# Turning y by transposes and taking two steps' router logits from four column groups

## The chip, the cores and the metric

The kernel runs on one core of a Trainium2 chip. The metric is the device time of one launch in microseconds (us); lower is better. The engines named below are PE (TensorE matmul; PEld is its weight load), DVE (VectorE), ACT (ScalarE), POOL (GpSimd) and SP (SyncE, which issues most DMAs here). Each engine works through its own queue strictly in the order in which the program was traced.

## The reference

An outer-product recurrence (the attention half) feeds a router with two experts of eight per token (the mixture half). All data are float32.

```python
# attention: B, H, S, D = 4, 8, 768, 48
f = 1 / (1 + exp(-f_logit))
for t in range(S):
    state = f[:, :, t, :, None] * state + einsum('bhd,bhe->bhde', k[:, :, t], v[:, :, t])
    y[:, :, t] = einsum('bhd,bhde->bhe', q[:, :, t], state)
x = y.transpose(0, 2, 1, 3).reshape(B * S, H * D)          # 3072 tokens x 384
# router: E = 8
noisy = x @ w_gate + log1p(exp(x @ w_noise)) * noise        # both weights 384 x 8
top2, weights = two largest of noisy, softmax over the two
# experts, hidden 1024
out[t] = sum over the two experts e of weight * (relu(x[t] @ w1[e]) @ w2[e])
```

## The kernel before, in words

**Attention.** The sequence is cut into 6 chunks of 128 tokens (`NCH`, `C`); with 4 batches this gives 24 steps, numbered n = 0 to 23. A step holds all 8 heads as 4 pairs (`HP`); a head has 48 features, padded to 64 (`DP`), so that a pair fills 128 partitions. A step's work is split into stages: `forget` (transpose f on PE, exp and log on ACT), `summed` (a running sum on DVE, tile `L`), `decays` (two exponentials on ACT), `scaled` (transpose q and k on PE, multiply on DVE), `scores` (transpose k back, score products on PE, mask on DVE, tile `A`), `output` (products `y`, new state) and `features`. The main loop runs the stages of different steps in turn, software-pipelined: iteration i does, in this order, `forget(i+3)`, `scaled(i+1)`, `scores(i)`, `summed(i+2)`, `output(i-1)`, `decays(i+2)`, `features(i-2)`. `in_order` pins each engine's queue to this order of tracing.

**Features before the change** (line 627 on). `output` leaves y with features on the partitions and tokens along the free side; ACT copies it out of the accumulation banks to `yT` (line 607). `features` multiplies each pair's 128 x 128 block of `yT` by `w_rt`, a 128 x 112 matrix for each pair: 96 columns of an identity (they turn y to token order) and 16 columns of router weights. One bank `xp` thus holds the turned x and four partial logits. DVE adds the four partial logits into `lg` (line 630), ACT copies the 384 columns of x to `xs` (line 632), and SP writes `xs` to `x_rows` in DRAM (line 633), from which tokens are later gathered by expert. The write is put into SP's queue in the `output` stage of the next iteration, behind the loads of f, q, k and v that the earlier stages of that iteration issue. `xs` has three buffers.

**Loads.** f, q, k and v go to rings of slots in SBUF (5, 4, 4 and 6 slots), several steps ahead: `scaled(n)` issues q and k of step n+3, `scores(n)` issues v of step n+3, `forget(n)` issues f of step n+4. From step 9 to 16 each iteration also issues a part of the first experts' weights.

**Router.** After the fourth step of a chunk c, `route(c)` is started: a chain of small operations on ACT and DVE, some of them between two of the loop's stages (`next(router)`), which finds the two best experts and each token's place in its expert's list (`sloti`, line 707). A small product on PE, `rk` (lines 697, 698), counts tokens ahead. Then POOL writes the list entries into DRAM, 8 indirect DMAs for each chunk (line 711).

**Hand-over.** In program order on POOL, the 8 list writes of the fourth chunk (c = 3, steps 12 to 15) are followed by the first gather of tokens (line 885), whose rows PE turns (`xgp`, line 922) before the first expert's products (line 977) can begin. The rest of the kernel is the experts' work: 8 experts in 24 groups of 256 tokens and five small blocks, with the first and second layers by fast matrix-product schemes.

**Banks.** Six accumulation banks go round among all uses of `one_bank`; a new use waits until the use six before it has been read.

Of the kernel before, what the change touches and what calls it, by code (L numbers as in the profile page):

```python
# [10 lines left out]
F32 = mybir.dt.float32  # L11
# [5 lines left out]
AX = mybir.AxisListType  # L17
ALU = mybir.AluOpType
# [314 lines left out]
def kernel(  # L333
# [38 lines left out]
    nc = tc.nc  # L372
    B, H, S, D = q.shape
    N, DM = out.shape
    E = moe_w_gate.shape[1]
    FF = moe_w1.shape[2]
    C = 128
    NCH = S // C
    HP = H // 2
    DP = 64  # L380
    KO = DM // 128
    FO = FF // 128
# [26 lines left out]
    const = ctx.enter_context(tc.tile_pool(name="const", bufs=1))  # L409
# [5 lines left out]
    wk = attention.enter_context(tc.tile_pool(name="wk", bufs=2))  # L415
# [3 lines left out]
    def one_bank(name):  # L419
        turns.append(turns.pop(0))  # L420
        return turns[-1].tile([128, 512], F32, tag="one", name=name)
# [5 lines left out]
    ident = const.tile([128, 128], F32, tag="ident", name="ident")  # L427
# [56 lines left out]


    XW = 2 * D
    w_rt = const.tile([128, HP, XW + 2 * E], F32, tag="w_rt", name="w_rt")
    noise = const.tile([128, NCH, B, E], F32, tag="noise", name="noise")

    def load_router(part):  # L490

        if part < 2:
            for i, w in ((part, (moe_w_gate, moe_w_noise)[part]),):
                for odd in range(2):
                    for par in range(2):
                        nc.gpsimd.dma_start(out=w_rt[par * DP:par * DP + D, odd::2, XW + i * E:XW + (i + 1) * E],
                                          in_=w.rearrange("(a o r d) e -> o r d a e", o=2, r=2, d=D)[odd, par ^ odd])
        else:
            c = part - 2
            nc.sync.dma_start(out=noise[:, c], in_=moe_noise.rearrange("(b s) e -> s b e", b=B)[c * C:(c + 1) * C])  # L500
# [15 lines left out]
    def cols(hp):  # L516
        return slice(hp * C, (hp + 1) * C)
# [62 lines left out]
    def output(n):  # L580
        c, b = n // B, n % B
# [18 lines left out]
        if c:  # L600
            for hp in range(HP):
                for par in range(2):
                    nc.tensor.matmul(at(hp, par), lhsT=state[b][rows(par), hp, :],  # L603
                                     rhs=qP[n][rows(par), cols(hp)], start=False, stop=(hp >= HP - 2))
        yT[n] = wk.tile([128, 2, HP // 2 * C], F32, tag="yT", name=f"yT_{n}")
        for odd in range(2):
            nc.scalar.copy(yT[n][:, odd, :], y[odd][:, 0:HP // 2 * C])  # L607
        if c == NCH - 1:
            return

# [4 lines left out]
        if c == 0:  # L615
            nc.gpsimd.tensor_tensor(new, dsv, end, ALU.mult)
        else:
            mid = wk.tile([128, HP, DP], F32, tag="mid", name=f"mid_{n}")
            nc.gpsimd.tensor_tensor(mid, dsv, state[b], ALU.add)
            nc.gpsimd.tensor_tensor(new, mid, end, ALU.mult)  # L620
        state[b] = new

    def features(n):
        c, b = n // B, n % B
        xp = one_bank(f"xp_{n}")[:, 0:HP * (XW + 2 * E)].rearrange("t (a w) -> t a w", a=HP)
        for hp in range(HP):
            nc.tensor.matmul(xp[:, hp, :], lhsT=yT[n][:, hp % 2, cols(hp // 2)], rhs=w_rt[:, hp, :], start=True, stop=True)  # L627
        if b == 0:
            lg[c] = rt.tile([128, B, 2 * E], F32, tag="lg", name=f"lg_{c}", bufs=NCH)
        nc.vector.tensor_reduce(lg[c][:, b, :], xp[:, :, XW:].rearrange("t a e -> t e a"), axis=AX.X, op=ALU.add)  # L630
        xs = wk.tile([128, HP, XW], F32, tag="xs", name=f"xs_{n}", bufs=3)
        nc.scalar.copy(xs, xp[:, :, 0:XW])
        xw.append(lambda: nc.sync.dma_start(out=x_rows[n * C:(n + 1) * C, :], in_=xs.rearrange("t a w -> t (a w)")))


    def route(c):
        def t(shape, tag, dtype=F32):
# [129 lines left out]
    def nearly_enough():  # L767
        total = one_bank("total_c")[:, 0:E]
        nc.tensor.matmul(total, lhsT=ones, rhs=upto[NCH - 2][:, :, B], start=True, stop=True)
        yield  # L770
        nc.vector.scalar_tensor_tensor(short, in0=total[0:1, 0:1], scalar=511.5, in1=short, op0=ALU.is_lt, op1=ALU.max)
        yield
# [646 lines left out]
    clamp(1, nc.vector)  # L1419
    pad("v")  # L1420
    nc.gpsimd.memset(w_rt, 0.0)
    for odd in range(2):
        for r in range(2):
            nc.gpsimd.tensor_copy(w_rt[:, odd::2, r * D:(r + 1) * D],
                                  ident[:, (r ^ odd) * DP:(r ^ odd) * DP + D].unsqueeze(1).broadcast_to((128, HP // 2, D)))
    for part in range(2):
        load_router(part)
    clamp(3)
# [67 lines left out]
    for i in range(-3, NS + 2):  # L1496
# [5 lines left out]
        for stage, lag in order:  # L1502
            n = i - lag
            if not 0 <= n < NS:
                continue
            stage(n)
            if stage is forget:
                for m in () if n < 2 else (n + 3,) if n < 5 else (n + 3, n + 4) if n == 5 else (n + 4,):
                    load("f", m)
# [48 lines left out]
        if n >= 0 and n % B == B - 1:  # L1558
            c = n // B
            router = chain(router, route(c))  # L1560
            n_routed = c + 1
            if c == HALF - 1:
                router = chain(router, enough())
                first_pairs = first_loads()
            if c == NCH - 1:
                router = chain(router, nearly_enough(), plan(), beyond())
    while NCH - 1 not in begun:
        next(router)
    for _ in first_pairs:
# [96 lines left out]
```

## Time and profile before

| | |
|---|---|
| median of three runs | 619.19 us (618.45 to 619.34) |
| profiled execution, its own time | 617.76 us |
| its span from first to last instruction | 615.7 us |
| PE busy | 602.0 us, 98% |
| DVE, ACT, POOL busy | 451.9, 377.8, 290.9 us (73, 61, 47%) |
| granted TensorE clock, mean | 0.996 |

The profile is one execution. Its own time lies 2.1 us above its span (launch and end around it), and 1.4 us below the median of the timed runs. Attention takes about the first 158 us. "Busy" counts instructions in flight; idle time of an engine is put down to the event that ended it, which is inferred.

### The profile page before, as it was taken

The numbers are of one execution on the slowest core, as the hardware profiler recorded it, in microseconds if no ns is written. First come the engines' busy times: TensorE is split into PE (matmuls) and PEld (weight loads), VectorE is DVE, ScalarE is ACT, GpSimd is POOL, SyncE is SP. The second block draws the span as 40 slices with busy tenths as digits, with TensorE's granted clock in tenths as the row PEclk, the third lists the DMA queues.
The fourth block names the chain that finished last, engine by engine and source line by source line (L and its number), as shares of the span: only waits on it lengthen the run. The fifth ranks groups of instructions, "written<-read, shape, count | busy, mean of one in ns | idle before, by whom it ended". The sixth has DMA issues, their size and how long they took to land.

```text
span 615.7 us, 13343 instructions
## 1 busy us (share of the span) xinstructions
PE 602.0 (98%) x4830; PEld 553.0 (90%) x4830; DVE 451.9 (73%) x1056; ACT 377.8 (61%) x920; POOL 290.9 (47%) x316
## 2 busy tenths in 40 slices
PE   8999999999999999999999999999999999999995
PEld 7999998887999988998898899889988998998994
DVE  7777878778665488878777778787777777877840
ACT  6877676754222587667666755775577567647611
POOL 7724688878887550451062335414540624242032
PEclk9999999999999999999999999999999999999998
DMA  9999887996973874686489279839874893361024
GB/s 185 187 200 213 174 173 158 206 190 162 327 193 87 142 195 138 142 165 212 138 196 263 65 197 170 259 136 185 159 215 128 199 250 84 82 136 20 2 27 56
DMA packets 186219, 98.79 MB, mean 160 GB/s; under 512 B 150736, under 2 KB 179408, under 8 KB 186144
## 3 DMA queue, kind: packets, MB, share of 16 engines
q1 hardware_dynamic: 173968, 78.59, 51.2%
q0 software_dynamic: 12176, 19.25, 17.2%
q8 instruction: 40, 0.66, 0.4%
q14 instruction: 35, 0.29, 0.2%
HBM read 69.68 MB, written 19.62 MB: 145 GB/s over the span
## 4 chain that ended last, share of the span: by engine, by line
PE 82%; DMA 6%; issue 3%; POOL 3%; ACT 2%; DVE 2%; POOLq 0%; ACTq 0%
PE y L1218 27%; PE E L1052 8%; PE D L1052 8%; PE B L1052 6%; PE C L1052 6%; PE hp L977 5%; PE y L1162 3%; DMA x_rows<-xs 3%; PE sc L574 3%; PE y L592 3%; PE xp L627 2%; PE A L1052 2%; DMA xg<-hs_b 2%; PE fp L534 1%; POOL lists L711 1%
## 5 line engine op out<-in xcount | busy, mean ns | idle before, releaser
L1099 POOL DMA_INDIRECT out_dram<-ys,slots x48 | 91.1, 1898 | 216.0 <-DVE ys L1224 167.6
L1218 PE MATMUL y<-qk_all,f_all 128*128 128x192 f32 x504 | 88.8, 326 | 0.0
L1218 PEld LDWEIGHTS y<-qk_all,f_all 128*128 128x128 f32 x504 | 83.1, 190 | 0.0
L885 POOL DMA_INDIRECT xg<-x_rows,slots x48 | 52.5, 1093 | 36.0 <-DMA slots<-lists 18.8
L1060 ACT ACTIVATE hs_b<-hs_b 128x256 f32<-128x256 f32 x140 | 58.5, 418 | 6.9 <-DVE hs_b L1064 5.2
L1224 DVE SCALAR_TENSOR_TENSOR ys<-y,slots,ys 128x192 f32<-128x192 f32 x63 | 26.1, 415 | 49.1 <-PE y L1218 16.4
L1218 PE MATMUL y<-w,hs_b 128*128 128x192 f32 x336 | 61.5, 326 | 0.0
L711 POOL DMA_INDIRECT lists<-entry,sloti x48 | 52.8, 1101 | 8.7 <-issue 7.4
L1218 PEld LDWEIGHTS y<-w,hs_b 128*128 128x128 f32 x336 | 56.0, 190 | 0.4
L1267 ACT ACTIVATE ys<-y,slots 128x192 f32<-128x192 f32 x21 | 8.9, 421 | 59.5 <-PE y L1218 55.7
L577 DVE TENSOR_TENSOR A<-sc,causal 128x1024 f32<-128x1024 f32 x24 | 29.3, 1221 | 9.0 <-PE sc L574 8.5
L607 ACT COPY yT<-y 128x256 f32<-128x256 f32 x48 | 15.7, 376 | 29.8 <-PE y L603 21.4
L1057 ACT COPY hs_a<-D 128x256 f32<-128x256 f32 x77 | 28.5, 371 | 8.4 <-PE D L1052 4.5
L1218 PE MATMUL y<-qk_all,hs_b 128*128 128x192 f32 x168 | 31.5, 331 | 0.3 <-ACT ys L1239 0.2
L936 ACT COPY planes<-xg 128x768 uint16<-128x768 uint16 x36 | 29.6, 825 | 3.4 <-DMA xg<-x_rows,slots 2.8
L1218 PE MATMUL y<-w,f_all 128*128 128x192 f32 x168 | 31.3, 329 | 0.0
L548 DVE TENSOR_TENSOR_SCAN L<-f,cap 128x512 f32<-128x512 f32 x24 | 29.3, 1221 | 1.4 <-ACT cap L543 1.4
L1057 ACT COPY hs_a<-E 128x256 f32<-128x256 f32 x63 | 23.5, 372 | 10.8 <-PE E L1052 9.5
L1218 PEld LDWEIGHTS y<-qk_all,hs_b 128*128 128x128 f32 x168 | 27.4, 190 | 3.0 <-issue 2.1
L528 POOL TENSOR_SCALAR f_all<-f_all 128x384 f32<-128x384 f32 x21 | 26.4, 1257 | 5.0 <-DMA f_all<-in_f_logit_dram 2.7
L1087 DVE TENSOR_TENSOR f_all<-hs_b 128x512 f32<-128x512 f32 x42 | 28.7, 682 | 0.0
L1218 PEld LDWEIGHTS y<-w,f_all 128*128 128x128 f32 x168 | 27.6, 190 | 0.7
(273 smaller groups left out, 1593.4 us busy)
## 6 DMA issues: line engine op xcount, KB each, us to landing
w<-in_moe_w_dram SPq DMA_DIRECT2D x12, 1536.0 KB
w_q<-in_moe_w_dram SPq DMA_DIRECT2D x10, 1536.0 KB
w<-in_moe_w_dram SPq DMA_DIRECT2D x16, 384.0 KB
f_all<-in_f_logit_dram SPq DMA_DIRECT2D x24, 192.0 KB
qk_all<-in_q_dram SPq DMA_DIRECT2D x24, 192.0 KB
qk_all<-in_k_dram SPq DMA_DIRECT2D x24, 192.0 KB
v_all<-in_v_dram SPq DMA_DIRECT2D x24, 192.0 KB
x_rows<-xs SPq DMA_DIRECT2D x24, 192.0 KB
```

The source lines that it names most:

```text
L548: nc.vector.tensor_tensor_scan(L[n], data0=logf[n], data1=cap[n % 2].rearrange("d a t -> d (a t)"), initial=0.0, op0=ALU.add, op1=ALU.min)
L577: nc.vector.tensor_tensor(A[n].rearrange("j r (a i) -> j (r a) i", i=C), sc.rearrange("j r (a i) -> j (r a) i", i=C), causal.unsqueeze(1). ...
L711: into = nc.gpsimd.indirect_dma_start(out=lists, out_offset=bass.IndirectOffsetOnAxis(ap=sloti[:, r, b:b + 1], axis=0), in_=entry[:, c, b, ...
L885: nc.gpsimd.indirect_dma_start(out=xg[p][:, s, :], out_offset=None, in_=x_rows[0:(known(p) + (p == 1 and s)) * B * C], in_offset=bass.Indi ...
L936: nc.scalar.copy(planes[p][:, s], by_halves(p)[:, s * 2 * DM:(s + 1) * 2 * DM].rearrange("t (d h) -> t h d", h=2))
L977: nc.tensor.matmul(hp[:, o, :], lhsT=w1[home(k)][:, i, (fo + o) * 128:(fo + o + 1) * 128], rhs=rows_of(k)[:, i, :], start=(i == 0), stop=( ...
L1052: nc.tensor.matmul(banks[name, j], lhsT=half_of(x, k)[:, j * 128:(j + 1) * 128], rhs=half_of(y, k), start=first, stop=True, skip_group_che ...
L1057: nc.scalar.copy(at(to, j), banks[more[0], j])
L1060: nc.scalar.activation(at(to, j), at(y, j), AF.Relu, scale=-1.0 if more[0][0] == "-" else 1.0)
L1087: nc.vector.tensor_tensor(sm[which], x, y, op)
L1099: into = nc.gpsimd.indirect_dma_start(out=out, out_offset=bass.IndirectOffsetOnAxis(ap=slots[p][:, s, 2:3], axis=0), in_=ys[s], in_offset= ...
L1218: nc.tensor.matmul(to, lhsT=x[:, o, :], rhs=y[:, o, :], start=(start and o == 0), stop=(o == FH - 1), skip_group_check=not start)
```

## The change

The turning matrix leaves `w_rt`, which shrinks to 32 columns for each pair (16 of weights, 16 of zeros). y is turned by four PE transposes for each step. The logits of an odd step and the even one before it are computed together: four products, one for each pair, with `w_rt` as the stationary operand and 256 columns of `yT` as the moving one; the four go to four groups of 32 partitions of one bank, `both`. DVE copies these 128 x 256 partial logits to SBUF (`parts`, a slice of `hs_a` that attention does not use otherwise); PE turns them back with two transposes, in `logits()`, which the main loop calls after the next stage that it runs; DVE then adds the pairs. `yT` becomes one tile for two steps. ACT writes `xs` in two copies. The buffer `mid` goes from two to one.

```diff
-    w_rt = const.tile([128, HP, XW + 2 * E], F32, tag="w_rt", name="w_rt")
+    EP = 32
+    w_rt = const.tile([128, HP, EP], F32, tag="w_rt", name="w_rt")
...
-        yT[n] = wk.tile([128, 2, HP // 2 * C], F32, tag="yT", name=f"yT_{n}")
+        if n % 2 == 0:
+            yT[n // 2] = wk.tile([128, HP, 2, C], F32, tag="yT", name=f"yT_{n}")
         for odd in range(2):
-            nc.scalar.copy(yT[n][:, odd, :], y[odd][:, 0:HP // 2 * C])
+            nc.scalar.copy(yT[n // 2][:, odd::2, n % 2, :], y[odd][:, 0:HP // 2 * C].rearrange("d (m t) -> d m t", t=C))
...
-            mid = wk.tile([128, HP, DP], F32, tag="mid", name=f"mid_{n}")
+            mid = wk.tile([128, HP, DP], F32, tag="mid", name=f"mid_{n}", bufs=1)
...
     def features(n):
         c, b = n // B, n % B
-        xp = one_bank(f"xp_{n}")[:, 0:HP * (XW + 2 * E)].rearrange("t (a w) -> t a w", a=HP)
-        for hp in range(HP):
-            nc.tensor.matmul(xp[:, hp, :], lhsT=yT[n][:, hp % 2, cols(hp // 2)], rhs=w_rt[:, hp, :], start=True, stop=True)
         if b == 0:
             lg[c] = rt.tile([128, B, 2 * E], F32, tag="lg", name=f"lg_{c}", bufs=NCH)
-        nc.vector.tensor_reduce(lg[c][:, b, :], xp[:, :, XW:].rearrange("t a e -> t e a"), axis=AX.X, op=ALU.add)
+        if n % 2:
+            both = one_bank(f"lg_{n}")
+            for hp in range(HP):
+                nc.tensor.matmul(both[hp * EP:(hp + 1) * EP, 0:2 * C], lhsT=w_rt[:, hp, :],
+                                 rhs=yT[n // 2][:, hp].rearrange("d b t -> d (b t)"), start=True, stop=True)
+            parts = hs_a[:, FO - 1, :]
+            nc.vector.tensor_copy(parts, both[:, 0:2 * C])
+            back.append((n, both, parts))
+        xp = one_bank(f"xp_{n}")
+        for hp in range(HP):
+            nc.tensor.transpose(xp[:, cols(hp)], yT[n // 2][:, hp, n % 2, :], ident)
         xs = wk.tile([128, HP, XW], F32, tag="xs", name=f"xs_{n}", bufs=3)
-        nc.scalar.copy(xs, xp[:, :, 0:XW])
+        blocks = xp.rearrange("t (m x d) -> t m x d", x=4, d=DP)
+        for to in range(2):
+            nc.scalar.copy(xs.rearrange("t (m o) (r d) -> t m o r d", o=2, r=2)[:, :, :, to, :],
+                           blocks[:, :, 0:4:3, 0:D] if to == 0 else blocks[:, :, 1:3, 0:D])
...
+    def logits():
+        n, both, parts = back.pop(0)
+        for b in range(2):
+            nc.tensor.transpose(both[:, (2 + b) * C:(3 + b) * C], parts[:, b * C:(b + 1) * C], ident)
+        nc.vector.tensor_reduce(lg[n // B][:, n % B - 1:n % B + 1, :],
+                                both[:, 2 * C:].rearrange("t (b a w) -> t b w a", b=2, w=EP)[:, :, 0:2 * E], axis=AX.X, op=ALU.add)
...
-    for odd in range(2):
-        for r in range(2):
-            nc.gpsimd.tensor_copy(w_rt[:, odd::2, r * D:(r + 1) * D],
-                                  ident[:, (r ^ odd) * DP:(r ^ odd) * DP + D].unsqueeze(1).broadcast_to((128, HP // 2, D)))
...
+            waiting = bool(back)
             stage(n)
+            if waiting:
+                logits()
...
+    logits()
     while NCH - 1 not in begun:
```

## Rows read from the trace of the kernel before

**Rows 1.** The page: busy time of each engine, its share of the span, instructions.

```profile
PE 602.0 (98%) x4830; PEld 553.0 (90%) x4830; DVE 451.9 (73%) x1056; ACT 377.8 (61%) x920; POOL 290.9 (47%) x316
```

**Rows 2.** The chain of work, one whole step in the middle of attention: start, length, engine, tile, line.

```profile
48.58 1.09 PE sc L574 x16
...
51.16 0.60 PE y L603 x16
51.76 1.07 PE xp L627 x8
52.83 0.44 PE fp L534 x4
...
54.58 1.09 PE sc L574 x16
```

**Rows 3.** The chain of work later, among the experts: four column groups of 32, stationary 128 x 32, moving 128 x 256, 12 products as 24 instructions.

```profile
301.75 1.43 PE hp_q L1317 x24
```

**Rows 4.** The chain of work from 96 to 160 us, the pieces that lead to the hand-over.

```profile
119.58 5.39 DMA x_rows<-xs
...
125.05 0.48 ACT xs L632
125.53 0.12 ACT ex L667
...
131.45 0.31 DVE sloti L707
...
132.03 1.01 POOL lists L711
...
145.14 3.73 DMA xg<-x_rows,slots
...
149.01 0.52 PE xgp L922 x3
```

**Rows 5.** Timeline of ACT, the copies to `xs` of steps 12, 14 and 16: start, length, then in brackets the idle time before and what ended it.

```profile
98.78 0.50 ACT L632 COPY xs<-xp 128x384 f32<-128x384 f32 x1
...
111.48 0.48 ACT L632 COPY xs<-xp 128x384 f32<-128x384 f32 x1 [0.77 <-DMA x_rows<-xs]
...
125.05 0.48 ACT L632 COPY xs<-xp 128x384 f32<-128x384 f32 x1 [1.47 <-DMA x_rows<-xs]
```

**Rows 6.** The tile `xs`, its copies and its writes to DRAM, up to 114 us: durations in ns (least, median, most), first and last start in us.

```profile
L632 ACT COPY xs<-xp x15: 468/497/499, 25.8 to 111.5; 128x384 f32<-128x384 f32 x15
L633 SPq DMA_DIRECT2D x_rows<-xs x13: 343/869/2542, 31.7 to 113.3; - x13
```

**Rows 7.** Loads of q issued up to 114 us, and transposes of q (four for a step) up to then.

```profile
L522 SPq DMA_DIRECT2D qk_all<-in_q_dram x20: 526/720/1908, 1.9 to 107.1; - x20
L534 PE MATMUL qp<-ident,qk_all x76: 272/273/328, 8.0 to 110.5; 128*128 128x128 f32 x76
```

**Rows 8.** Timeline of SP's queue around the write of step 13 to `x_rows`.

```profile
118.79 0.70 SPq L522 DMA_DIRECT2D v_all<-in_v_dram  x1
119.58 0.66 SPq L633 DMA_DIRECT2D x_rows<-xs  x1
```

**Rows 9.** Waits of SP's queue from 0 to 165 us, the largest entry: total, times, longest.

```profile
SPq L522 <- PE y L603: 6.8, 5, 2.7
```

**Rows 10.** Two stretches: length, busy time (and count) of PE, PEld, DVE, ACT, POOL, then the granted clock, the DMA engines' busy share, GB/s.

```profile
25.00:98.00 73.00, 72.39 (x1039) 66.13 (x1037) 55.33 (x131) 53.38 (x144) 43.76 (x64) 1.00 0.89 186
118.00:131.00 13.00, 12.58 (x180) 11.12 (x181) 9.84 (x35) 8.67 (x24) 10.29 (x16) 1.00 1.02 224
```

**Rows 11.** Timeline of DVE from 129 us: the running sum, the logits of step 17, and the router's operation behind them.

```profile
129.29 1.21 DVE L548 TENSOR_TENSOR_SCAN L<-f,cap 128x512 f32<-128x512 f32 x1
130.42 0.20 DVE L630 TENSOR_REDUCE lg<-xp 128x16 f32<-128x64 f32 x1
130.53 0.18 DVE L701 TENSOR_TENSOR at<-rk,list_of 128x32 f32<-128x32 f32 x1
```

**Rows 12.** Single lines with their durations in ns: a copy out of a bank by DVE, 384 and a sum of 192 columns; a reduction over 128 columns; a copy out of a bank by ACT, 256 columns, and a scaled one of 192.

```profile
L923 DVE COPY xt_a<-xgp x2: 545/546/548, 150.3 to 152.6; 128x384 f32<-128x384 f32 x2
L1192 DVE TENSOR_TENSOR mid<-mid,y x3: 353/354/354, 174.6 to 216.4; 128x192 f32<-128x192 f32 x3
L794 DVE TENSOR_REDUCE ex_plan<-past_plan x1: 285/285/285, 175.1 to 175.1; 128x16 f32<-128x128 f32 x1
L607 ACT COPY yT<-y 128x256 f32<-128x256 f32 x48 | 15.7, 376 | 29.8 <-PE y L603 21.4 <-PE kp L534 3.4 <-PE qp L534 3.1
L1243 ACT ACTIVATE ys<-y,slots 128x192 f32<-128x192 f32 x21 | 8.8, 421 | 9.4 <-PE y L1218 9.3
```

**Rows 13.** Timeline of PE from 127 us (start, length in flight, line), and at the hand-over.

```profile
127.45 1.63 PE L627 MATMUL xp<-w_rt,yT 128*128 128x112 f32 x8
128.92 0.32 PE L697 MATMUL rk<-each,earlier 128*128 128x32 f32 x2
...
129.30 0.63 PE L534 MATMUL fp<-ident,f_all 128*128 128x128 f32 x4
...
149.01 0.52 PE L922 MATMUL xgp<-ident,xg 128*128 128x128 f32 x3 [0.80 <-DMA xg<-x_rows,slots]
```

More of the change, by code (lines that the diff above doesn't have):

```diff
@@ L495, in load_router @@
                     for par in range(2):
-                        nc.gpsimd.dma_start(out=w_rt[par * DP:par * DP + D, odd::2, XW + i * E:XW + (i + 1) * E],
+                        nc.gpsimd.dma_start(out=w_rt[par * DP:par * DP + D, odd::2, i * E:(i + 1) * E],
                                           in_=w.rearrange("(a o r d) e -> o r d a e", o=2, r=2, d=D)[odd, par ^ odd])
@@ L624, in features @@
         c, b = n // B, n % B
-        xp = one_bank(f"xp_{n}")[:, 0:HP * (XW + 2 * E)].rearrange("t (a w) -> t a w", a=HP)
-        for hp in range(HP):
-            nc.tensor.matmul(xp[:, hp, :], lhsT=yT[n][:, hp % 2, cols(hp // 2)], rhs=w_rt[:, hp, :], start=True, stop=True)
         if b == 0:
             lg[c] = rt.tile([128, B, 2 * E], F32, tag="lg", name=f"lg_{c}", bufs=NCH)
-        nc.vector.tensor_reduce(lg[c][:, b, :], xp[:, :, XW:].rearrange("t a e -> t e a"), axis=AX.X, op=ALU.add)
+        if n % 2:
[9 more added lines that the diff above has]
+            nc.tensor.transpose(xp[:, cols(hp)], yT[n // 2][:, hp, n % 2, :], ident)
         xs = wk.tile([128, HP, XW], F32, tag="xs", name=f"xs_{n}", bufs=3)
-        nc.scalar.copy(xs, xp[:, :, 0:XW])
+        blocks = xp.rearrange("t (m x d) -> t m x d", x=4, d=DP)
+        for to in range(2):
+            nc.scalar.copy(xs.rearrange("t (m o) (r d) -> t m o r d", o=2, r=2)[:, :, :, to, :],
+                           blocks[:, :, 0:4:3, 0:D] if to == 0 else blocks[:, :, 1:3, 0:D])
         xw.append(lambda: nc.sync.dma_start(out=x_rows[n * C:(n + 1) * C, :], in_=xs.rearrange("t a w -> t (a w)")))
+    back = []
+    def logits():
[4 more added lines that the diff above has]
+                                both[:, 2 * C:].rearrange("t (b a w) -> t b w a", b=2, w=EP)[:, :, 0:2 * E], axis=AX.X, op=ALU.add)
     def route(c):
```

## Prediction

> **What bounds the kernel now.** The page comes first: PE is busy for 98% of the span [rows 1], so any PE time saved looks like time saved. The chain of work in mid-attention says the same: one step runs from one score product to the next, 48.58 to 54.58, 6.00 us of PE work without a gap, with 1.07 for the four products of `features` [rows 2].
>
> But a busy share does not tell what *starts* the expert work. For that I read the chain that leads to the hand-over [rows 4]. It does not run along PE. It runs: a write of `x_rows` that lands at 124.97 (119.58 + 5.39); ACT's copy to `xs` at 125.05, which had waited for that landing because `xs` has three buffers; the router's exponential (`ex`) behind it on ACT; a run of DVE work to `sloti` at 131.76; eight list writes on POOL back to back; the first gather; and at 149.01 PE turns the gathered rows, after an idle 0.80 us [rows 13]. So PE is already 0.80 us *early* there. What PE saves ahead of 149 can only make this wait longer, unless the chain itself moves. The timeline of ACT agrees: from step 14 on, copies to `xs` begin with 0.77 to 1.47 us of waiting for a landing [rows 5].
>
> Does that landing move when PE gets faster? Up to 114 us there are 15 copies to `xs` and 13 writes of them [rows 6]: the thirteenth copy (step 12) starts at 98.78 [rows 5], its write goes out at 113.3 [rows 6]. SP is 14 us behind its data. Its loads are late in the same way: the twentieth load of q, issued at 107.1, needs the ring slot of the sixteenth q (four slots), yet the nineteenth q is being turned at 110.4 [rows 7] and a step is 6 us, so that slot was free some 12 us earlier. The write of step 13, the one that lands at 124.97, goes out at 119.58, 0.09 after the load ahead of it ends at 119.49 [rows 8]. SP thus waits for neither PE nor ACT; it is held by its own transfers, whose engines are busy at a share of 0.89 from 25 to 98 us and 1.02 from 118 to 131 [rows 10]. The view of SP's waits does name PE (6.8 us in all [rows 9]), but it names the last event before an issue; by the count of slots the slot had long been free. I conclude that the landing at 124.97 is paced by the transfers.
>
> **The change part by part.**
>
> *PE.* Removed, for two steps: 2 x 1.07 = 2.14 us. Added: eight transposes at 0.11 (0.44 for four [rows 2]) = 0.88; two turning back, 0.22; four products in column groups. The same form, 128 x 32 stationary and 256 columns moving, takes 1.43 us for 12 products among the experts [rows 3], so a third, 0.48; a single group of four may show its start-up, 0.58 at most (two passes of 256 columns at the 0.107 of a 128-column pass each, 0.43, plus the 0.15 by which 1.43 exceeds three times that). I take 0.53. A pair of steps then costs 1.63, and PE saves 0.51, twelve times: 6.1 us, of which 8 pairs, 4.1 us, lie ahead of step 16.
>
> The Trainium skill, "TensorE: Matmul & The Clock Gate", Part 4 on PE-mode transpose, gives about 275 ns for a transpose in a kernel. The trace agrees with that for one in flight (272 to 328 ns [rows 7]) but starts one every 110 ns [rows 2]. By the page's figure ten transposes would take 2.75 us, the pair 3.28, and PE would lose 1.14 us a pair; by the row it saves 0.51. I go by the row.
>
> *Ahead of 124.97.* Since nothing here moves the landing, all that PE, DVE and ACT win or lose before it is priced at nothing; the cover is ACT's 1.47 us of waiting [rows 5], and without it every microsecond of PE's lead or lag would count. That covers the four POOL copies into `w_rt` that go, the strided copies to `yT` (256 columns as before), the single `mid` (its two users follow each other on POOL anyway) and the extra bank `both` (read before the use six later, which stands behind twelve transposes and the score products, 1.32 + 1.09 us [rows 2]).
>
> *From 124.97 to `sloti`.* Here the change adds links:
> 1. `xs` in two copies stands ahead of `ex` on ACT. 256 columns take 0.376 [rows 12], 384 take 0.48 [rows 5]; by that slope 192 take 0.32, two 0.64: +0.16. Bounds: 0 (the columns are the same), and two scaled 192-column operations at 0.421 [rows 12], +0.36.
> 2. On DVE the reduction of step 17 starts at 130.42 and the router's `at` follows at 130.53, 0.11 later [rows 11]. Now DVE copies 256 columns there: between 0.354 (192) and 0.546 (384) [rows 12], 0.42, of which 0.1 overlaps the next, as the running sum's 1.21 lets the next start after 1.13 [rows 11]. 0.35 in place of 0.11: +0.24 (0.15 to 0.35).
> 3. `at` comes after `logits()`, so DVE now waits while PE turns the parts back. PE stands ready: its f transposes end by about 129.9 before, and the copy ends at 130.9. Three such transposes take 0.52 from first start to last end [rows 4], two about 0.41; with 0.02 to 0.05 at each hand-over, 0.5 (0.35 to 0.8).
> 4. The reduction, now over 128 columns: 0.285 [rows 12], less the overlap 0.2 (0.2 to 0.3).
>
> Sum 0.16 + 0.24 + 0.5 + 0.2 = **+1.1** at `sloti`. Behind it POOL's list writes and the gather follow back to back, 132.03 to 149 [rows 4], so the turn on PE is 1.1 later. Meanwhile PE is held in step 17: queued behind the two back transposes are the next q and k transposes and all else. It would have reached them at 127.45 + 0.53 + 0.44 + 0.24 (`rk`) + 0.44 = 129.1 and waits until about 131, 1.9. Its lead pays, and four more steps at 0.25 win half of that back before 149; the gather is still later.
>
> *After the hand-over.* The logits of step 21 are turned back ahead of `rk` of chunk 4: +0.22. Step 23 costs 0.53 + 0.44 + 0.22 in place of 1.07, +0.1, and step 22's 0.63 is lost to the wait on the turned rows: 0 to 0.2 in all, 0.18 taken. Together **+0.4** (0 to 0.5). From there PE is full and everything moves along.
>
> Profiled time 617.76 + 1.5 = 619.3; the profiled execution lies 1.4 below the median of the runs, so on the median 619.19 + 1.5 = **620.7**. All bounds low give +0.7, all high +2.3; the runs themselves spread over 0.9. Range of this case alone: 619.4 to 621.9.
>
> **The rivals.**
>
> *A: the landing moves with PE (faster).* If SP is paced by ring slots after all, as the view of its waits says [rows 9], then PE's lead, at most 4.1 us at step 16 and less where DVE comes late to its copy (I take 3.0), moves the landing. With the +1.5 this is -1.5; if writes then also stop holding ACT, another 1.47 goes: -3.0. I take -2.2: 617.0. It decides from a lead passed on of 1.5 us up. Against it: the 14 us by which SP trails.
>
> *B: PE is the bound throughout.* 6.1 less the 1.7 to 1.9 us that it waits in step 17: -4.4, 614.8. For it: 98% [rows 1]. Against it: PE's wait at 149.01 [rows 13].
>
> *C: the shared `yT` couples the steps (slower).* In one iteration ACT writes step n+1 into the tile just before PE reads the even step n from it. If that read waits for the write (the halves interleave), PE stands for two copies, 2 x 0.376 + 0.05 = 0.8, in nine even steps up to 16: 7.2 less the saved 4.1, less ACT's 1.47 of cover, is 1.6; with the 1.5, +3.1: 622.3. The halves do not touch, which speaks against it.
>
> *D: the transposes slow PE.* If each waited for the one before to end (0.273 in flight [rows 7]), a pair would cost 2.73 + 0.53 = 3.26 in place of 2.14, and eight pairs would put PE 9 us late at step 16; less 1.47, with 1.5, 628. The granted clock is 1.00, the 2.4 GHz level, throughout attention [rows 10], where 16 transposes a step already run. The Trainium skill's same Part 4 says that transposes do not count as activity for the clock as other work does; no run here shows a loss of clock by it.
>
> **How the numbers follow.** A change under 0.2%, 1.24 us, cannot be told from none here. Forecast 0.60 (slower 0.36, same 0.23, faster 0.01); A 0.20 (faster 0.16, same 0.04); B 0.07; C 0.11; D 0.02. Sums: faster 0.24, same 0.27, slower 0.49. The range 616.4 to 622.9 leaves out B, D, and the ends of A and C, under 0.2 together.
>
> **What would show it.** Right: SP's writes of steps 12 and 13 still go out near 113 and 119.5 and ACT waits longer for them; on DVE a gap before the reduction of step 17; `sloti` of chunk 3 near 132.9; PE's idle time before `xgp` near 1 us or more at about 150; a step of 5.75 us in mid-attention. Wrong: those writes go out earlier, and `sloti` before 131 (A); no wait before `xgp` (B); PE waiting for ACT's `yT` copies in even steps (C); transposes starting more than 0.11 apart (D).

## The result: 5 us slower, and the profile after

The changed kernel takes 624.13 us (median of 8 runs, 620.51 to 625.92) against 618.49 (8 runs, 617.99 to 619.34) for the kernel before beside it: a ratio of 1.0082 with a 95% interval of 1.0055 to 1.0109. In two later comparisons it was 1.0058 (1.0025 to 1.0092) and 1.0052 (1.0022 to 1.0082). The three intervals share 1.0055 to 1.0082, 3.4 to 5.1 us. The forecast of 620.7 had the direction right and the size wrong; the time lies outside its range. (By the two later ratios it would be 622.4 to 622.8, at the range's upper end.) Nearly all single runs of the kernel before lay between 615 and 629 in these and the comparisons below, where the three that the forecast had spread over 0.9 us; so only the medians of many runs, with their intervals, can show such differences.

The profiled execution of the changed kernel took 625.92, 624.2 of it span. Its page answers to [rows 1]; below it is the line with the granted clock in 40 slices, which was 9 in all slices of attention before:

```profile
PE 603.2 (97%) x4854; PEld 546.7 (88%) x4854; DVE 456.8 (73%) x1056; ACT 378.2 (61%) x944; POOL 286.8 (46%) x312
PEclk9999989999999999999999999999999999999998
```

PE is no less busy than before (603.2 against 602.0), and one slice of attention, 78 to 94 us, shows an 8. The chain of work in mid-attention, where nothing waits, answers to [rows 2]; start, length, piece:

```profile
37.87 0.60 PE y L604 x16
38.47 0.57 PE lg L632 x8
39.04 0.59 PE xp L639 x4
...
40.06 0.22 PE lg L653 x2
...
44.77 0.59 PE xp L639 x4
...
49.68 0.60 PE y L604 x16
50.28 0.57 PE lg L632 x8
```

Two steps, from `y` at 37.87 to `y` at 49.68, take 11.81 us, where [rows 2] gives 2 x 6.00. The change saves 0.19 us a pair, not 0.51.

The time is lost where PE waits. First the sum by instruction, from 20 to 165 us (total, times, longest), then PE's timeline at steps 9, 15 and 19 (a step is named here by its `features`); brackets hold the idle time before and what ended it:

```profile
PE lg L653 <- DVE hs_a L635: 4.9, 4, 1.9
```

```profile
74.40 0.64 PE L632 MATMUL lg<-yT,w_rt 128*32 128x256 f32 x8
74.97 0.66 PE L639 MATMUL xp<-ident,yT 128*128 128x128 f32 x4
75.47 0.60 PE L535 MATMUL fp<-ident,f_all 128*128 128x128 f32 x4
77.97 0.44 PE L653 MATMUL lg<-ident,hs_a 128*128 128x128 f32 x2 [1.91 <-DVE hs_a L635]
...
119.85 0.44 PE L653 MATMUL lg<-ident,hs_a 128*128 128x128 f32 x2 [1.26 <-DVE hs_a L635]
...
146.98 0.44 PE L653 MATMUL lg<-ident,hs_a 128*128 128x128 f32 x2 [1.54 <-DVE hs_a L635]
```

PE comes to the two transposes back and DVE has not yet copied what they turn. Two further profiles of the same kernel have 3.2 us (3 waits) and 3.9 us (3 waits). Step 9 is among them each time (1.9, 1.9, 1.7); the others move about (13, 15, 17, 19).

Step 9 has its cause on DVE. Its timeline, and GpSimd's (POOL) beside it:

```profile
73.95 1.21 DVE L549 TENSOR_TENSOR_SCAN L<-f,cap 128x512 f32<-128x512 f32 x1
...
75.79 1.09 DVE L701 TENSOR_TENSOR each<-hot 128x32 f32<-128x32 f32 x1
76.81 0.16 DVE L710 COPY each<-upto 128x8 f32<-128x8 f32 x1
77.01 0.59 DVE L714 TENSOR_TENSOR_SCAN upto<-carry,each 128x40 f32<-128x40 f32 x1
77.52 0.39 DVE L635 COPY hs_a<-lg 128x256 f32<-128x256 f32 x1
```

```profile
76.07 0.73 POOL L621 TENSOR_TENSOR mid<-dss,st 128x256 f32<-128x256 f32 x1
76.89 0.62 POOL L622 TENSOR_TENSOR st<-mid,P 128x256 f32<-128x256 f32 x1
```

The column products end at 75.0, but the copy stands behind the running sum and the router's operations and starts at 77.52. Two of those operations are stretched: `each` (0.21 before) takes 1.09 and ends as POOL's `mid` ends, `upto` (0.24 before) takes 0.59 and ends as `st` ends. In the kernel before POOL idled while this `each` ran (77.45; `mid` began at 77.90); a later one, at 149.01, took 0.56 there and ended as POOL's `st` ended (149.57, 149.51). The Trainium skill, "GPSIMD Engine Reference", 1. Specifications, says that GpSimd shares its SBUF interfaces with VectorE and contends with its instructions that have two SBUF inputs; `each` and the scan `upto` are such instructions, and the trace agrees.

At steps 15 and 19 DVE is not busy: it waits, by the view for PE. DVE's timeline:

```profile
119.37 0.42 DVE L635 COPY hs_a<-lg 128x256 f32<-128x256 f32 x1 [1.63 <-PE fp L535]
```

The products for this copy (PE 116.93, 0.64) end at 117.57, the copy starts 1.8 us later; the `fp` named in the bracket had ended at 118.59. So PE's signal comes late, or something holds DVE that the trace does not show. Such starts, about 2 us behind PE's products, are in the kernel before too: ACT's copies to `yT` at 96.84 and 140.62, whose `y` products ended at 94.72 and 138.68, had idled 3.1 and 3.4 us. The first of them cost PE 0.61 us, the second nothing that PE's waits list. What delays them stays open.

After the first wait the clock fell. Two stretches: length, busy time and count of PE, PEld, DVE, ACT, POOL, then granted clock, DMA share, GB/s:

```profile
75.00:78.00 3.00, 1.09 (x13) 0.86 (x9) 2.78 (x9) 2.97 (x9) 2.76 (x5) 1.00 0.93 216
80.00:82.00 2.00, 2.00 (x17) 1.79 (x16) 0.24 (x1) 0.59 (x1) 1.66 (x3) 0.50 1.03 216
```

PE was idle for 1.91 us of the first, and in the second the grant is 0.50, the 1.2 GHz level; the score products at 80.14 took 2.01 instead of 1.09, the `kp` transposes ahead of them 0.85 instead of 0.44. Ahead of the fall PE had run only transposes since 75.47, on either side of the idle time. The other two profiles of this kernel, with much the same wait at step 9, show no fall there: from the `fp` of that step to the next `fp` they take 8.50 and 8.18 us, this one 9.97. So the fall is not the whole loss; it made this execution some 1.5 us longer.

Last, the hand-over. DVE's `sloti` of chunk 3, then PE (compare [rows 4, 13]):

```profile
135.18 0.17 DVE L728 CAST sloti<-slot 128x8 uint32<-128x8 f32 x1
```

```profile
154.76 0.49 PE L943 MATMUL xgp<-ident,xg 128*128 128x128 f32 x3
...
160.00 2.83 PE L998 MATMUL hp<-xt_a,w 128*128 128x256 f32 x12 [0.81 <-DVE xt_a L944]
```

`sloti` is 3.7 us later than before, the first product of the experts (`hp`; 153.22 before) 6.8. From `hp` to the end of the span it is 464.2, before 462.5. In the other two profiles `sloti` comes at 134.33 and 135.25, `hp` at 158.22 and 157.38, and the rest is 463.2 and 463.7. Most of the loss is made ahead of the experts.

What made `sloti` late is seen on ACT and DVE. ACT's copies ahead of the router's last chain, in the first profile and in the third, then DVE's chain in the first (compare [rows 5, 11]):

```profile
125.96 0.65 ACT L609 COPY yT<-y 128x256 f32<-128x256 f32 x2 [3.36 <-PE xp L639]
...
127.89 0.56 ACT L643 COPY xs<-xp 128x192 f32<-128x192 f32 x2
```

```profile
127.98 0.54 ACT L643 COPY xs<-xp 128x192 f32<-128x192 f32 x2 [2.51 <-DMA x_rows<-xs]
```

```profile
132.14 1.21 DVE L549 TENSOR_TENSOR_SCAN L<-f,cap 128x512 f32<-128x512 f32 x1
...
134.20 0.29 DVE L654 TENSOR_REDUCE lg<-lg 128x32 f32<-128x128 f32 x1 [0.53 <-PE lg L653]
```

The copy to `xs` that started at 125.05 before starts at 127.89, 127.03 and 127.98, and DVE's running sum is late by the same 2.0 to 2.9 us. In the first two profiles none of ACT's copies to `xs` waits for a landing; ACT comes late because its copies to `yT` had waited for PE (3.36 and 3.95 us). In the third it is the landing that is late, 127.90 against 124.97, and ACT waits five times for one (10.2 us). From the running sum to `sloti` it is then 3.04 us in all three, 2.16 before.

### The profile page after: what moved, and what is told of

Read it like the earlier page. It is cut to its first block, busy times and chain, and to the rows that moved or that the text cites. A ratio compares the mean times of both kernels' runs of the same rounds, so it can differ in the third digit from the quotient of the medians.

```text
span 624.2 us, 13419 instructions
## 1 busy us (share of the span) xinstructions
PE 603.2 (97%) x4854; PEld 546.7 (88%) x4854; DVE 456.8 (73%) x1056; ACT 378.2 (61%) x944; POOL 286.8 (46%) x312
## 4 chain that ended last, share of the span: by engine, by line
PE 89%; DVE 5%; issue 2%; POOL 1%; SPq 1%; DMA 1%; ACT 0%; POOLq 0%; DVEq 0%
PE y L1239 29%; PE E L1073 8%; PE D L1073 8%; PE B L1073 6%; PE C L1073 6%; PE hp L998 4%; PE sc L575 4%; PE y L1183 4%; PE y L593 3%; PE A L1073 2%; PE xp L639 2%; PE kp L535 2%; PE y L604 2%; PE qp L535 2%; PE fp L535 1%
## 5 line engine op out<-in xcount | busy, mean ns | idle before, releaser
L732 POOL DMA_INDIRECT lists<-entry,sloti x48 | 51.2, 1067 | 15.2 <-issue 7.7
L575 PE MATMUL sc<-qP,kQ 64*128 64x128 f32 x384 | 28.8, 291 | 0.3 <-DVE A L578 0.3
```

The source lines that it names most:

```text
L575: nc.tensor.matmul(sc[:, par, cols(hp)], lhsT=kQ[n][rows(par), cols(hp)], rhs=qP[n][rows(par), cols(hp)], start=True, stop=True)
L732: into = nc.gpsimd.indirect_dma_start(out=lists, out_offset=bass.IndirectOffsetOnAxis(ap=sloti[:, r, b:b + 1], axis=0), in_=entry[:, c, b, ...
```

## Experiments

The theory at the start, W: PE loses time at the round trip through DVE. Its rival, V: the loss is in the column-group products, the dense transposes, or signals that are late by chance. A third view is the forecast's own: PE's place ahead of the hand-over counts for nothing until a cover is used up. Each ratio is against runs of the kernel before made beside it, whose medians were 619.4 to 621.8.

**The changed kernel again.** 

> The changed kernel once more, for a second profile beside the others. 623 to 625 us by both theories. Theory W (TensorE loses its lead where it waits for the copy that VectorE makes between the column-group products and the two transposes back): four or so of the 12 waits longer than 0.3 us again, 4 to 5 us together, and the first product of the hp tile near 160 us, not 153. Theory V (the loss is in the column-group products, the dense transposes or in signals that come late by chance): the waits stand at other steps, with another sum, and the time follows them.

1.0058; waits of 3.2 us in all, at steps 9 and 15 above all, `hp` at 158.22. That is near W's picture. 

> The changed kernel in the same call as e9_later_again: 3 to 6 us above the kernel before; waits at the transposes back of 3 to 5 us in all, at other steps than in the two profiles so far where they come from late signals, at step 9 again where they come from VectorE's queue.

1.0052; waits of 3.9 us at steps 9, 13 and 17. But this execution is not W's alone: PE is on time at step 12 (95.46 against 95.63) in spite of the wait at step 9, then waits 2.5 us for loads of k, and the late landing sets `sloti`. Whether the change delays the landing or chance does, no run shows; the longest run of a later kernel (e11_late_to_13), with that landing ahead of a copy at 128.83, has it too.

**The round trip later.** The turning back moves behind the scores and into a bank of its own, and the router's steps of a chunk begin two places later:

```
         n, both, parts = back.pop(0)
+        both = one_bank(f"lb_{n}")
...
-            if waiting:
+            if waiting and (stage is scores or i >= NS):
                 logits()
```

> The changed kernel with the two transposes back put behind the stage of the scores instead of behind the stage of the forget gate (2.4 us of TensorE's own work lies between instead of 0.44), in a bank of their own; the router's steps of a chunk begin two places later and their first pause is two places shorter. Theory W: no wait at the transposes back, the granted clock stays at 1.00 around 80 us, the first product of hp comes 6 to 8 us earlier, at 152 to 154 us, and the time is 616 to 618.5. Theory V: the waits turn up at other instructions and the time stays at 622 or more. The argument of the forecast, that what TensorE gains ahead of the hand-over ends in a wait for the gathered rows: TensorE idles 1 us or more before the first transpose into xgp and the time is 619 to 620.7.

1.0004 (0.9966 to 1.0042); `sloti` at 131.55, `hp` at 154.82. PE's largest waits, 20 to 165 us:

```profile
PE kp L535 <- ACT yT L609: 1.7, 2, 1.0
PE hp L1001 <- DVE xt_a L947: 1.1, 1, 1.1
```

The wait at the transposes back is gone (0.3 us is left, at one place) and the granted clock stays at 9 in the page's slices of attention; the loss goes with them. But the kernel isn't faster than before either, where W had 616 to 618.5. 

> The kernel of e1_later again with more rounds. Theory W and TensorE's real saving of 0.19 us per pair (12.00 to 11.81 between the forget gate's transposes in mid-attention): 0 to 2 us below the kernel before, 3 to 6 us below the changed kernel of this call. If something else of the change costs as well: 1 us or more above the kernel before.

1.0011 (0.9981 to 1.0042), `sloti` 131.51, `hp` 153.99. Against the changed kernel beside it the median is lower by 1.8 us the first time (621.65, 623.44) and by 1.7 the second (619.86, 621.59); by the ratios it is 3.3 and 2.5. W is borne out for the loss, with these numbers for its size. The small gain of 0.19 a pair cannot be seen; why is told below (e4_no_logits). No run moves the router's steps alone; but e10_late_from_15 below has them moved too, keeps the early trips, and keeps their waits (1.67 at step 9, 0.98 at step 13).

**One stage later, and at once.** Same edit with `stage is scaled`, in the old bank, the router's steps one place later; and, in the other run, `logits()` called directly behind `features`. 

> The changed kernel with the two transposes back one stage later (behind the transposes of q and k, same bank, 1.8 us of TensorE's own work between), the router's steps begin one place later with a first pause one shorter. Theory W: long waits lose 0.87 us each; 1 to 2 us of waits are left of 4 to 5, and the time lies between the changed kernel and the run three stages later (e1_later), 1 to 3 us below the changed kernel. If it is the extra bank or ScalarE's copies that make TensorE late: no better than the changed kernel.

1.0017 (0.9996 to 1.0038). 

> The changed kernel with the two transposes back right behind the transposes of x: 0.49 us of TensorE's own work between the column-group products and them instead of 0.93. Theory W (TensorE waits for VectorE's copy): a wait of 0.2 to 0.5 us at each of the 12 places and the few long ones longer, 4 to 6 us more than the changed kernel in the same call, 627 to 630. If the wait is not the cause: the same time as the changed kernel.

1.0111 (1.0067 to 1.0154), `sloti` 138.17, `hp` 163.31. PE's waits at the transposes back, first of the one, then of the other:

```profile
PE lg L653 <- DVE hs_a L635: 1.7, 3, 1.2
PE lg L653 <- issue: 1.6, 1, 1.6
```

```profile
PE lg L653 <- DVE hs_a L635: 7.6, 8, 1.7
PE lg L653 <- DVE L L549: 1.5, 1, 1.5
```

With PE's own work between products and turning back at 0.49, 0.93, 1.8 and 3.4 us (counted from the end of the products, so with the transposes of x), the ratio goes 1.0111, 1.0052 to 1.0082, 1.0017, 1.0004 to 1.0011. That is one ordered series, as W has it, though the intervals of neighbours overlap. (The profile of the third, one stage later, is of the longest of its runs, 624.39.)

**The trip alone, on the kernel before.** The first form let the copy begin after the features' second product:

```
+            if n % 2 and hp == 1:
+                parts = hs_a[:, FO - 1, :]
+                nc.vector.tensor_copy(parts[:, 0:2 * (XW + 2 * E)].rearrange("t (a w) -> t a w", a=2), xp[:, 0:2, :])
+                back.append((n, parts))
...
+            nc.tensor.transpose(trip[0:96, b * C:(b + 1) * C], parts[:, b * C:b * C + 96], ident)
```

> The kernel before, with a round trip added that carries nothing of the result: in odd steps VectorE copies 224 columns of the features' bank to SBUF after its second product, and TensorE turns two blocks of that copy back after the next stage's four transposes (0.22 us of TensorE and 0.6 us of VectorE per pair). Theory W: TensorE waits at those transposes as in the changed kernel and the kernel before becomes 4 to 7 us slower, 622.5 to 625.5. Theory V: only the added work counts, part of it under ScalarE's slack, 618.5 to 620.5.

1.0235, but for another reason: the third product, into the same bank, waited for the copy (9.6 us at 11 places, named so in PE's waits). It tells nothing of the trip. The second form copies after all four products:

> The kernel before with a round trip that carries nothing of the result, this time copied after the features' fourth product, so that no product waits for the copy: in odd steps VectorE copies 224 columns of that bank to SBUF, and behind the forget gate's four transposes TensorE turns two blocks of the copy back (0.22 us of TensorE and some 0.6 us of VectorE per pair; 0.44 us of TensorE's own work lies between). Theory W: a wait in nearly every odd step, 0.2 to 1 us, 4 to 9 us in all, and with the 2.6 us of added transposes 6 to 11 us more than the kernel before. If waits of this kind cost nothing: 1 to 3 us more.

1.0097 (1.0066 to 1.0127), `hp` at 161.21, 8 us later than before. PE's waits:

```profile
PE trip L646 <- DVE lg L634: 2.9, 4, 1.0
PE trip L646 <- DVE L L548: 0.6, 1, 0.6
...
PE trip L646 <- DVE hs_a L630: 0.3, 1, 0.3
```

A round trip costs at least as much on the old kernel as the change does, with none of its other parts. The waits at the turning back come to 3.8 us, a little under W's 4 to 9. At step 17 PE is 5.6 late (the forget-gate transposes behind its features at 134.93 against 129.30). Ahead of that lie four of the listed waits, 2.4 us, and eight added pairs of transposes, 1.8. The other 1.4 are partly stops too short for the list: step 5, which has no listed wait, takes 6.53 us instead of 6.00, 0.3 more than its pair.

**No round trip.** x by transposes, the logits of each step from four products of 16 columns:

```
...
+        for hp in range(HP):
+            nc.tensor.matmul(xp[:, D:D + 2 * E], lhsT=yT[n // 2][:, hp, n % 2, :], rhs=w_rt[:, hp, 0:2 * E],
+                             start=(hp == 0), stop=(hp == HP - 1))
```

> x by transposes as in the change, but the logits of each step from four small products (16 columns each, summed in PSUM) in the spare columns of the same bank, and read by one copy on VectorE as before: no column groups, nothing turned back. By the rows TensorE needs per pair of steps 0.88 for the transposes and 0.5 to 0.9 for the small products, 1.4 to 1.8 instead of 2.14. Theory W: no waits, 0.35 to 0.75 us gained per pair, first hp product at 149 to 152 us, time 613.5 to 617. Theory V with the transposes as the cause: 621 or more. The forecast's argument (gain ends in the wait for the gathered rows): 618 to 620.

1.0092 (1.0057 to 1.0126). My sum was wrong; of W this run shows only that the waits go with the trip. PE's timeline:

```profile
53.43 0.66 PE L631 MATMUL xp<-ident,yT 128*128 128x128 f32 x4
53.93 0.96 PE L633 MATMUL xp<-w_rt,yT 128*128 128x16 f32 x8
54.74 0.64 PE L535 MATMUL fp<-ident,f_all 128*128 128x128 f32 x4
```

The four small products run as eight passes, one every 0.10 us, nearly as long as passes of 112 columns (0.12): 0.81 a step where I had put 0.25 to 0.45. `features` takes 1.31 a step instead of 0.98, and the run is one of plain lateness, 0.36 a step (from `fp` to `fp` 6.36 us instead of 6.00), without any wait of PE above 0.3.

**Lateness by a known dose.** A product that nobody reads, in steps 0 to 16 of the kernel before, once and twice:

```
+        if n < 17:
+            nc.tensor.matmul(bank[:, 448:512], lhsT=yT[n][:, 0, cols(0)], rhs=ident[:, 0:64], start=True, stop=True)
```

> The kernel before with one more product on TensorE in each of the steps 0 to 16 (64 columns, two passes, 0.22 us, into spare columns that nobody reads): a known lateness of 3.7 us by step 17 and no wait for another engine. The forecast's cover (1.47 us of ScalarE's waiting, 0.80 us of TensorE's): 1.4 to 2.2 us of it arrive, first hp product at 154.6 to 155.5. Theory W, that lateness of TensorE arrives whole: 3.5 us or more, hp at 156.5 or later.

0.9996 (0.9969 to 1.0023): nothing arrives. 

> The kernel of e8_dose with two such products in each of the steps 0 to 16, 0.44 us or a little more per step, some 7.5 us by step 17. If about 3 us are taken up and the rest arrives: sloti of chunk 3 near 135 to 136, first hp product at 157.5 to 159, 4 to 5 us above the kernel before. If lateness of TensorE alone never reaches the hand-over: within 1 us of the kernel before.

1.0077 (1.0046 to 1.0107), 4.8 us. PE at the hand-over, one dose and two:

```profile
150.19 0.52 PE L925 MATMUL xgp<-ident,xg 128*128 128x128 f32 x3 [0.89 <-DMA xg<-x_rows,slots]
...
154.40 2.86 PE L980 MATMUL hp<-xt_a,w 128*128 128x256 f32 x12 [0.26 <-DVE xt_a L926]
```

```profile
153.59 0.52 PE L926 MATMUL xgp<-ident,xg 128*128 128x128 f32 x3 [0.55 <-DMA xg<-x_rows,slots]
...
157.81 2.86 PE L981 MATMUL hp<-xt_a,w 128*128 128x256 f32 x12 [0.27 <-DVE xt_a L927]
```

With one dose PE is 2.8 us late at step 12 (the forget-gate transposes behind its features at 98.41 against 95.63) and 1.1 at step 17 (130.43 against 129.30): the kernel before has stops of its own from step 12 on (from there to step 13 it takes 7.34 us, from step 16 to 17 7.32), and a PE that is late in this way meets fewer of them (6.22 and 6.38). With two, 5.6 and 4.9 us, and it arrives. So there is a cover for plain lateness, some 3 us (7.5 added, 4.8 arrive), and the forecast's 1.47 was if anything too small.

**PE ahead instead of late.** 

> The changed kernel with the router's logits left out: x by transposes, no column-group products, no copy, nothing turned back; the logits are set to zero, so that the noise alone routes, and the rest runs as it is. TensorE then has 0.49 us less per step than the kernel before (features to forget gate 0.49 instead of 0.98), 9 us by step 18. If TensorE's place in the steps sets the hand-over in both directions: first hp product at 143 to 146 us and a time 7 to 10 us below the kernel before of the same call. If the landing of x_rows sets it, as the forecast argued: TensorE stands 1 us or more ahead of xgp and the time is 0 to 3 us below. The difference to the changed kernel is what the new way to the logits costs in all.

Only the stretch up to 131 us is read; with other logits the work behind it is another. PE runs ahead as it should, 6.1 us by step 12 (89.51 against 95.63), and then stands:

```profile
99.37 0.63 PE L535 MATMUL kp<-ident,qk_all 128*128 128x128 f32 x4 [2.11 <-DMA qk_all<-in_k_dram]
...
126.68 0.88 PE L593 MATMUL y<-A,v_all 128*64 128x128 f32 x12 [1.20 <-ACT xs L636]
```

```profile
98.00:110.00 12.00, 10.63 (x100) 9.45 (x102) 5.62 (x11) 5.90 (x17) 6.20 (x11) 0.72 0.81 163
```

It waits for loads of k and q and for ACT, which waits for a write of `x_rows`; after the 2.11 us of idling the granted clock is 0.72 over 12 us, partly the 1.2 GHz level; by step 17 the lead is gone (129.75 against 129.30) and `sloti` comes at 132.59. A lead of PE is not kept, as the forecast argued, though it is ACT's copies, held by landings (PE waits 0.99 us for one at 94.52), and loads of k and q that stop it first, not the gathered rows. SP's writes bear it out: over all profiles the one of step 12 goes out between 107.5 and 116.8, at 113.3 in the kernel before, at 112.5 in e4 with its lead, and earliest in e2 with its late PE.

**One link of the forecast's chain.** Four buffers (`bufs=4`) for `xs` in the kernel before. 

> The kernel before with four buffers for xs instead of three, nothing else: ScalarE's copies no longer wait for the landing of an earlier write of x_rows. The forecast's chain (landing, copy to xs, ex, sloti, lists, gather, turn): sloti of chunk 3 comes 1.0 to 1.5 us earlier than 131.5, TensorE's wait of 0.80 us before xgp goes, and the kernel gains 0.8 to 1.5 us. If TensorE's own place in the steps sets the hand-over (theory W): no difference beyond 0.5 us.

1.0001 (0.9968 to 1.0034), `sloti` 130.79, `xgp` 148.79. The gain by the forecast's chain does not come. ACT no longer waits for a landing and `sloti` is 0.7 earlier, but PE now meets late loads of k (2.5 us at two places) and the hand-over moves by 0.2. As far as this profile shows, the landing was one of several limits that lie close together.

**Which waits count.** The later place from step 15 on alone, and (with `n < 15`) up to step 13 alone; the router's steps begin two places later in both:

```
+    def moved_back(n):
+        return n >= 15
...
+            if waiting and back and (stage is scores or i >= NS or not moved_back(back[0][0])):
```

> The changed kernel with the turning back left where it is up to step 13, and put behind the scores (as in e1_later) from step 15 on. By e8_dose some 3 us of lateness are taken up before step 17. Theory W2 (only what makes TensorE late in steps 15 and 17 reaches sloti of chunk 3): as e1_later, sloti near 131.5 to 132.5, 0 to 1.5 us above the kernel before. If every wait counts alike: 2 to 3 us above.

1.0019 (0.9983 to 1.0056), `sloti` 132.37. 

> The mirror image: behind the scores up to step 13, and where the change has it from step 15 on. Theory W2: as the changed kernel, sloti of chunk 3 near 134 to 135, 3 to 5 us above the kernel before. If every wait counts alike: 1.5 to 2.5 us above.

1.0019 (0.9986 to 1.0052). The profiled execution of the second, at 627.10 the longest of its twelve, with `sloti` at 137.34, is no guide to its median, 621.63. Theory W2, that only late steps count, isn't borne out: both halves lie between the whole and nothing. The intervals are too wide to say more.

**The queue ahead of the copy.** The router's pauses of chunk 1 move, nothing else (one tuple of a longer line):

```
-(3, 1, 1, 1, 1, 1, 2, 1, 1, 5, 1, 1)
+(3, 1, 1, 1, 1, 1, 4, 1, 1, 3, 1, 1)
```

> The changed kernel, with the router's operations of chunk 1 from sm on two places later (its seventh pause 4 instead of 2, its tenth 3 instead of 5), so that each and upto stand behind VectorE's copy of step 9 and not ahead of it. If the wait of step 9 comes from VectorE's queue, with each and upto held to 1.09 and 0.59 us while GpSimd works on mid and st: the wait at the transposes back of step 9 falls from 1.9 to under 0.3 us, the time goes 0 to 2 us down from the changed kernel's 3 to 5 above the kernel before. If TensorE's signal is what comes late there: the wait stays above 1.2 us.

1.0029 (1.0002 to 1.0057). DVE's copy of step 9, then PE's turning back:

```profile
76.12 0.42 DVE L635 COPY hs_a<-lg 128x256 f32<-128x256 f32 x1
```

```profile
76.59 0.44 PE L653 MATMUL lg<-ident,hs_a 128*128 128x128 f32 x2
...
132.59 0.44 PE L653 MATMUL lg<-ident,hs_a 128*128 128x128 f32 x2 [1.33 <-DVE hs_a L635]
```

The wait of step 9 is gone; one at step 17 is left, and PE's other waits are for ACT's copies and for loads. So step 9 was DVE's queue. The median, 622.09, is 1.4 us below one of the changed kernel's (623.44), which is not clear of the noise. That the stretched `each` and `upto` are POOL's doing rests on their ends in the trace; no run took POOL away.

## Why the prediction was wrong

**PE's saving, 0.51 a pair: wrong size.** The column groups (0.53 forecast, 0.57 measured) and the two back (0.22, 0.22) were right. The transposes of x were costed at 0.11 each, 0.88 for eight; in the chain a group of four takes 0.59, behind the `y` products and behind the column groups alike, 0.15 of it start-up, so 1.18. The 1.07 of the old products held a start-up too (from start to start they take 0.98). I had taken the 0.44 of `fp`, which follows other transposes, for a group that doesn't. Sum 1.97 against 2.14, and by whole steps 0.19.

**"All that PE, DVE and ACT win or lose before it is priced at nothing": the step that failed.** Its reasoning held in both directions it looked at. SP's pace does not follow PE, a lead is not kept (e4), and a plain lateness of 3.7 us is covered (e8). What it did not do is list the waits that the change puts on PE ahead of step 17. I looked at the round trip in step 17 alone, where I had it at 1.9; the same trip stands in all odd steps. There the copy stands in DVE's queue behind the scores' mask, the running sum and the router, and at some steps it starts 1 to 2 us behind PE's products with DVE idle, as ACT's copies do in the kernel before with little harm. The waits, 3 to 5 us a profile with a fall of the clock in one, come to 3.2, 3.1 and 2.7 us ahead of step 17's own trip, and in two profiles ACT's 1.47 of waiting is gone: its copy to `xs` starts 2.8 and 2.0 us late and waits for no landing. At step 17 itself the trip, for which I had 1.9, held PE for 0, 0.17 and 1.29 us. In the third profile it is the landing, which I took to stay at 124.97, that came 2.9 later.

**"+1.1 at `sloti`": the links were right.** `sloti` came 2.9 to 3.8 us later, 2.0 to 2.9 of it because the copy to `xs` and the running sum began late. From the running sum on the links add 0.88 in each of the three profiles (3.04 against 2.16), where the forecast's three have 0.24 + 0.5 + 0.2 = 0.94. By pieces: DVE's gap ahead of the reduction 0.53 for 0.5, the copy 0.42 and the reduction 0.29 as forecast. The two copies of `xs` take 0.56 instead of 0.48, half of the 0.16, and none of that is seen at the running sum.

**From `sloti` to the end.** To `hp`, where the forecast let all follow back to back, it takes 3.1, 2.1 and 0.4 us more than before. In the first profile PE, held 1.54 at step 19, comes to `xgp` when the rows are there; in the second the gather takes 5.53 instead of 3.73. From `hp` to the end it is 0.7 to 1.7 more, forecast +0.4 after the hand-over.

**The signs.** SP's writes of steps 12 and 13, first profile:

```profile
109.10 1.34 SPq L645 DMA_DIRECT2D x_rows<-xs  x1
...
118.73 0.59 SPq L645 DMA_DIRECT2D x_rows<-xs  x1
```

Forecast near 113 and 119.5, measured 109 and 119, in the other two 110 and 119, 115 and 121: within what the write of step 12 does from kernel to kernel. ACT waiting longer for them: in the third profile alone. PE idle before `xgp` by 1 us or more: 1.50 and 1.02 in two profiles, none in the first. A gap on DVE before the reduction of step 17: 0.53 in all three. A step of 5.75: 5.91. `sloti` near 132.9: 134.3 to 135.3.

**The rivals.** None came. A and B asked for a gain from PE's lead; e4 shows that there is none to be had. C named a coupling between steps, at ACT's copies, not at DVE's. D asked for slow transposes; they start 0.11 apart. The clock fell after idling with only transposes on either side; whether they have a share in the fall, no run shows. The case that happened stood in the text as "PE is held in step 17", its price paid by a lead that was two thirds smaller.

**Still open.** Why e8's 3.7 us cost nothing and the change's 3 to 5 us of waits cost nearly all. Seen from step 12 to 13 and from 16 to 17, e8 meets no stop (6.22, 6.38) and the changed kernel mostly does (8.05, 7.31, 6.08; 7.42, 8.36, 8.42). A reason is argued only: a wait in the trip also holds DVE, which stands idle while PE turns back (0.53 at step 9, ahead of the reduction) with the next step's work behind it, while a dose on PE holds only PE. Open too is what lets DVE and ACT start late behind PE's products, and what made the landing late in the third profile.

## What to carry to other kernels

A result that goes from TensorE to another engine and back is priced by the queue of that other engine at that place, in every step where it stands, and not by the length of its copy; put as much of TensorE's own work between as that queue is long (here 0.93 us left 3 to 5 us of waits, 3.4 us left at most 0.3). Cost a removed and an added group by the same view, with the start-up behind the same neighbour. Before counting on cover, test it with a plain dose: one and two doses showed where it ends for plain lateness, and a version with work left out showed that a lead was worth nothing. And take several profiles: here the same kernel was held by TensorE in two and by a landing in the third.

## What the runs showed of the hardware

TensorE's granted clock went to 0.50 after 1.91 us of idling, with only transposes on either side, in one execution, and stayed at 1.00 after 1.88 and 1.67 in two others of the same kernel. Small f32 products cost by the pass: 16 columns took 0.10 us a pass, 112 columns 0.12 (0.98 for eight). Two operations of DVE with two SBUF inputs, of 0.2 us, took 0.59 and 1.09 beside POOL's `st` and `mid` and ended as these ended. With PE late by more than the cover, runs spread less: two doses 623.4 to 626.2, the kernel before beside it 615.7 to 627.1.
